# A fused linear-attention and two-layer kernel: the inputs of its first two groups laid out as token pairs, with tiled matmuls and a new hand-written order

## The chip, the cores and the metric

The kernel runs on one core of one Trainium2 chip. The metric is the device time of one launch in microseconds. Before the change three runs took 174.21, 173.97 and 174.07 us, median 174.07 us.

The engines are named as the profile names them: PE (matrix engine, with PEld for its weight loads), DVE (vector), ACT (scalar), POOL (GpSimd) and SP, which here only issues DMAs. Each engine runs its own queue of instructions strictly in order and waits on semaphores for the others.

## The reference

Two layers in a row. The first is a linear attention with a decaying state; for each batch `b`, head `h` and token `t`:

```python
B, H, S, D = 4, 8, 768, 48
for t in range(S):
    cur = einsum('bhd,bhe->bhde', u * k[t], v[t])
    y[t] = einsum('bhd,bhde->bhe', r[t], state + cur)
    state = w[:, :, None] * state + einsum('bhd,bhe->bhde', k[t], v[t])
```

`w` lies between 0.85 and 0.95, one value for each head and channel. The second layer takes `x`, the 3072 tokens with their 8 * 48 = 384 channels, through

```python
h = x @ w_in                       # 384 -> 2048
g = where(h >= 1, h, where(h <= -1, 0, (h + 1) ** 2 / 4))
out = g @ w_out                    # 2048 -> 384
```

All inputs and the output are float32 in DRAM; the matmuls run in bf16.

## The kernel before, in words

The tokens are cut into chunks of C = 128. A **unit** is one chunk of one batch, and a **group** is two units: the same chunk of two batches. There are 12 groups, g = 0 to 11, in order of chunk; groups 0 and 1 are chunk 0 of batches 0, 1 and of batches 2, 3. Unit n = 2g + j. Groups 0 and 1 have no state to read, since theirs is the first chunk.

For each group the attention is done in the chunked form. R, K and V are loaded with the token on the partition (`LR`, `LK`, `LV`, line 253), one 192-byte run for each token and head. `Rs` and `Ks` are R and K times powers of w (tables `Wup` and `Wdn`), in bf16; they are transposed, on PE for the first units (`TR`, `TK`, `T`) and by a DMA transpose later (`RT`, `KT`); `A` multiplies the transposes to 128 x 128 scores for each head; `AT` masks them with a triangular table on DVE; `Y` multiplies the masked scores by V and adds the state's part. The token's own term goes through `KU`, `RKU`, the sum `us` and the product `B`. `y` adds the two. `Sp`, `Tm`, `decayg` and `sbf` carry the state on. The result is transposed again, on PE (`X`, `xc`) for groups 0 to 2 and by a DMA transpose `xcg` (tile `xT`, line 467) from group 3.

The second layer runs in quarters q of 512 hidden channels for each group: `m g.q` is 12 matmuls into a pair of PSUM banks (tile `hp`, line 475), `r`, `s` (ACT, a few `r` on DVE) and `g` (DVE) are the activation, and `M g.jq` is four matmuls of unit j into the output's PSUM tile `op` (line 512). `og` copies a group's `op` to the SBUF tile `o` (line 112), which has four buffers, and `stg` stores it (line 558).

**What sets the order.** A long table of words, `ORDER`, is run through from left to right, and each engine's queue is the order in which the words issue its instructions; nothing reorders them later. `Z` words are matmuls on zeros whose result nobody reads (tile `z`, line 566); there are 60 of them. All loads, the DMA transposes and the stores are issued from SP in the order of the words; the weights `w_in` and `w_out` (`WI`, `WO`) are issued from POOL. PSUM is eight banks: two pairs `p0` and `p1` and, for the first two groups, four single banks, which become the pairs `p2` and `p3` later. A tile in a pair waits until the last reader of the pair's earlier tile is done.

The lines by which the steps below can be found: loads 253, DMA transposes 318 (`RT`, `KT`) and 467 (`xT`), scores 370, `Y` 432 and 438, `m` 475, `M` 512, copies of any kind 112, stores 558, and for the last group 539 and 555.

```python
def do_stg(e, b, g):
    nc.sync.dma_start(out=rows_out(g, 0, UNITS), in_=tiles["o", g])
```

Of the kernel before, what the change touches and what calls it, by code (L numbers as in the profile page):

```python
# [15 lines left out]
P = 128  # L16
# [23 lines left out]
M3.13 M3.03 xcg4 m4.0/1 LR7 KU5=G RKU5=G AT10 LK7 decayg3=G sbfg3=A Rs6=G og3=A us5 LV7 B5=G KU6=G RKU6=G r4.0 Sp8/2  # L40
Sp9 AT11 Tmg4 m4.1/3 s4.0=A Y10/0 Y11 yg5 m4.2/2 r4.1 g4.0 xcg5 RT6 s4.1=A g4.1 m4.3/0 r4.2 us6 KT6 r4.3 LV8 s4.2=A
g4.2 M4.00/1 M4.10 M4.01 stg0 M4.11 s4.3=A g4.3 m5.1/3 Ks7=G V7 M4.12 LR8 decayg4=G Rs7=G AA6/02 M4.02 M4.03 M4.13
r5.1 AT12 m5.0/0 s5.1=A V6 sbfg4=A stg2 AT13 Y12/2 Y13 stg1 og4=V m5.2/1 g5.1 KU8=G B6=G yg6 m5.3/3 KT7 xcg6 Sp10/2
r5.0 s5.0=A KU7=G RKU7=G r5.2 s5.2=A Sp11 g5.0 M5.00/0 M5.10 M5.11 M5.01 RT7 Tmg5 LR9 g5.2 M5.02 Ks8=G LK9 us7 r5.3
s5.3=A V8 g5.3 decayg5=G sbfg5=A LK11 m6.1/2 r6.1 s6.1=A stg3 Rs8=G RT8 B7=G AA7/13 M5.03 Rs9=G M5.12 M5.13 AT15
m6.0/3 og5=A r6.0 AT14 g6.1 Y14/0 Y15 yg7 RKU8=G KU9=G xcg7 s6.0=A m6.3/1 m6.2/2 g6.0 Sp12/0 Sp13 r6.3 r6.2 s6.2=A us8
KT8 M6.00/3 M6.10 M6.11 M6.01 Tmg6 LV11 B8=G s6.3=A m7.1/0 RT9 LK10 g6.2 M6.02 LV10 g6.3 AA8/21 M6.03 r7.1 M6.12 M6.13
decayg6=G AT16 sbfg6=A RKU9=G LR10 s7.1=A AT17 Ks9=G og6=A m7.0/2 Sp14/1 Sp15 Y16/3 Y17 r7.0 g7.1 m7.2/0 KU11=G s7.0=A
Tmg7 yg8 xcg8 Ks10=G KT9 r7.2 m7.3/1 g7.0 M7.00/3 s7.2=A g7.2 M7.10 M7.11 LV9 r7.3 M7.01 KU10=G s7.3=A g7.3 V10 stg6
decayg7=G M7.12 RKU10=G sbfg7=A M7.02 AA9/02 M7.13 m8.0/1 stg5 LR11 AT18 Rs10=G V9 KT10 M7.03 r8.0 s8.0=A AT19 RT10  # L50
og7=V us9 B9=G m8.1/0 m8.2/2 r8.1 s8.1=A Y18/3 Y19 stg7 g8.0 m8.3/1 yg9 r8.2 Rs11=G RKU11=G M8.00/3 M8.10 xcg9 g8.1
M8.11 s8.2=A g8.2 Sp16/0 Sp17 Tmg8 stg4 RT11 r8.3 s8.3=A M8.01 M8.02 g8.3 m9.0/2 r9.0 s9.0=A us10 decayg8=G AA10/01
AT21 Ks11=G M8.03 sbfg8=A B10=G AT20 M8.12 M8.13 g9.0 og8=A m9.1/1 Y20/0 Y21 r9.1 m9.2/3 s9.1=A yg10 xcg10 g9.1 r9.2
M9.00/0 m9.3/2 KT11 s9.2=A stg8 M9.10 M9.11 Sp18/1 Sp19 r9.3 g9.2 s9.3=A M9.01 Tmg9 M9.02 g9.3 m10.0/3 decayg9=G V11
us11 AA11/12 B11=G r10.0 s10.0=A AT23 M9.12 M9.03 M9.13 AT22 m10.1/2 g10.0 sbfg9=A Y22/1 Y23 og9=A r10.1 stg9 s10.1=A
yg11 xcg11 m10.3/0 M10.00/3 g10.1 M10.10 r10.3 m10.2/1 s10.3=A g10.3 r10.2 M10.11 M10.01 s10.2=A m11.0/2 g10.2 r11.0
# [18 lines left out]
def kernel(  # L75
# [82 lines left out]
    )  # L158
    wCm = const.tile([P, NP, 2 * D], F32, name="wCm")
# [53 lines left out]
    def do_Wup(e, b):  # L213
        t = tiles["up_t"] = pair(b[0], F32, "up_t")[:, 0, :DM]
        nc.scalar.activation(t, flat(tiles["lwp"]), AF.Exp, scale=up_col)

    def do_Wdn(e, b):
        t = tiles["dn_t"] = bank(b[0], [P, DM], F32, "dn_t")
        nc.scalar.activation(t, flat(tiles["lwp"]), AF.Exp, scale=dn_col)
# [30 lines left out]
    def load(x, what, cls, g, j):  # L250
        j0, j1 = by_unit(g, j)
        t = make(cls, (what, g), [P, UNITS * H, D], F32)
        nc.sync.dma_start(out=t[:, j0 * H : j1 * H, :], in_=source(x, g, j0, j1))
# [38 lines left out]
    def do_KU(e, b, g, j=None):  # L292
        product(e, make("KU", ("KU", g), [P, UNITS * H, D], F32), tiles["K", g], u_sb, g, j)
# [317 lines left out]
```

## Time and profile before

| | |
|---|---|
| median of three runs | 174.07 us (173.97 to 174.21) |
| span of the profiled execution, first to last instruction | 172.6 us |
| outside the span, by the median | about 1.5 us |
| PE busy | 164.4 us, 95% of the span, 1674 matmuls |
| DVE, ACT, POOL busy | 130.6, 129.9, 117.4 us |
| moved by DMA | 28.26 MB in 103,751 packets |

The page gives no other time for the profiled execution than its span, so sums are made against the span, and the 1.5 us around it are taken as unchanged. The page's first part is the busy time of each engine; the second cuts the span into 40 slices of 4.3 us; the third lists the DMA queues (q1 is SP's, q10 is ACT's, q0 is POOL's); the fourth follows the chain of work that ended last back from the end; the fifth groups instructions by line. Timelines give start and duration, then engine, line, operation and operands, and in brackets how long the engine stood idle before and what ended that.

### The profile page before, as it was taken

Reading aid. Unit: us, or ns where it says so; the run is one execution under the profiler, and the core shown is the slowest. Engines: PE = TensorE matmul, PEld = TensorE weight load, DVE = VectorE, ACT = ScalarE, POOL = GpSimd, SP = SyncE. Lnnn points to the kernel's source line nnn. Section 1 sums busy time; section 2 is a strip of 40 time slices with the busy share of each in tenths; the row PEclk is TensorE's granted clock in tenths of the full one; section 3 lists DMA queues with packets and bytes.
Section 4 is the critical chain, followed back from the end, with each engine's and each line's share of the span. In section 5 each row is a group of like instructions: output and inputs, shape, how many; then the busy total and the mean of one; then the engine's idle time right before and its main releaser. Section 6 shows DMA issues by size and latency. Waiting matters only on the chain.

```text
span 172.6 us, 4051 instructions
## 1 busy us (share of the span) xinstructions
PE 164.4 (95%) x1674; PEld 132.9 (77%) x1674; DVE 130.6 (76%) x150; ACT 129.9 (75%) x150; POOL 117.4 (68%) x86
## 2 busy tenths in 40 slices
PE   7989968999999999989999999999999999999991
PEld 5769868966889777588787797696897787888871
DVE  4578698988687688859789779885889959873752
ACT  4355698991699899189979879689695896988940
POOL 3496744998689949999999998999568804300000
PEclk9999999999999999999999999999999999999999
DMA  6999999998996999999999997998999025140022
GB/s 114 194 184 179 199 187 180 228 210 174 206 191 99 206 184 168 194 199 145 196 312 210 182 220 163 223 182 155 297 170 267 4 52 145 37 104 0 8 91 91
DMA packets 103751, 28.26 MB, mean 164 GB/s; under 512 B 98866, under 2 KB 102836, under 8 KB 103732
## 3 DMA queue, kind: packets, MB, share of 16 engines
q1 hardware_dynamic: 101824, 24.75, 79.9%
q0 software_dynamic: 1760, 3.15, 9.8%
q8 instruction: 13, 0.21, 0.6%
q10 hardware_dynamic: 148, 0.10, 0.2%
q14 instruction: 6, 0.05, 0.1%
HBM read 20.45 MB, written 4.72 MB: 146 GB/s over the span
## 4 chain that ended last, share of the span: by engine, by line
PE 87%; ACT 4%; DMA 2%; DVE 2%; issue 1%; POOL 0%; ACTq 0%; DVEq 0%
PE hp L475 35%; PE op L512 34%; PE A L370 4%; PE Y L438 3%; DMA xT<-y 2%; PE Y L432 2%; PE Sp L405 2%; PE z L566 2%; ACT pt L486 1%; PE T L330 1%; ACT TT L112 1%; PE lwp L207 1%; PE wp L233 1%; PE TR L330 1%; PE TK L330 1%
## 5 line engine op out<-in xcount | busy, mean ns | idle before, releaser
L475 PE MATMUL hp<-xT,w_in 128*128 128x256 bf16 x576 | 69.1, 273 | 1.3 <-DMA xT<-y 0.8
L512 PE MATMUL op<-w_out,g 128*128 128x384 bf16 (+1 forms) x400 | 68.4, 320 | 0.0
L498 DVE SCALAR_TENSOR_TENSOR g<-sq,hp 128x1024 bf16<-128x1024 bf16 x48 | 57.9, 1215 | 13.2 <-ACT sq L495 13.2
L475 PEld LDWEIGHTS <-w_in 128*128 128x128 bf16 x576 | 61.9, 114 | 4.6 <-issue 1.6
L486 ACT ACTIVATE pt<-hp 128x1024 f32<-128x1024 f32 x46 | 46.9, 1021 | 13.7 <-PE hp L475 13.7
L512 PEld LDWEIGHTS <-g 128*128 128x128 bf16 x400 | 37.5, 98 | 20.4
L495 ACT ACTIVATE sq<-pt 128x1024 bf16<-128x1024 f32 x46 | 48.3, 1057 | 1.2
L379 DVE TENSOR_TENSOR AT<-A,umask 128x1024 bf16<-128x1024 f32 x20 | 23.7, 1220 | 5.2 <-PE A L370 5.2
L282 POOL TENSOR_TENSOR Ks<-Ki,Wdn 128x768 bf16<-128x768 f32 (+1 forms) x12 | 20.3, 1689 | 8.5 <-ACT Wdn L225 3.4
L313 POOL TENSOR_TENSOR V<-Vb,diag 128x768 f32<-128x768 bf16 (+1 forms) x14 | 18.1, 1291 | 9.8 <-DVE diag L304 4.4
L282 POOL TENSOR_TENSOR RKU<-Ri,KU 128x768 f32<-128x768 f32 (+1 forms) x13 | 21.2, 1630 | 1.1 <-DVE KU L282 0.7
L282 POOL TENSOR_TENSOR KU<-Ki,u_sb 128x768 f32<-128x768 f32 (+1 forms) x13 | 21.2, 1634 | 0.4 <-DMA Ki<-in_k_dram 0.4
L416 POOL TENSOR_TENSOR state<-Tm,wCm 128x768 f32<-128x768 f32 x8 | 14.6, 1824 | 9.8 <-DVE Tm L413 9.8
L282 POOL TENSOR_TENSOR Rs<-Ri,Wup 128x768 bf16<-128x768 f32 x10 | 18.2, 1820 | 0.3 <-DMA Ri<-in_r_dram 0.3
L112 ACT CAST Vb<-Vi 128x768 bf16<-128x768 f32 (+1 forms) x14 | 10.2, 733 | 5.4 <-DMA Vi<-in_v_dram 5.4
L450 DVE TENSOR_TENSOR y<-Y,V 128x768 bf16<-128x768 f32 x10 | 9.6, 956 | 5.9 <-PE Y L438 3.3
L304 DVE TENSOR_REDUCE diag<-RKU 128x16 f32<-128x768 f32 (+1 forms) x14 | 11.6, 831 | 1.5 <-POOL RKU L282 1.5
L112 ACT CAST state_bf<-state 128x768 bf16<-128x768 f32 (+1 forms) x12 | 8.5, 717 | 4.4 <-POOL state L416 4.4
L112 ACT COPY o<-op 128x768 f32<-128x768 f32 (+1 forms) x9 | 6.7, 748 | 6.0 <-PE op L512 5.9
L438 PE MATMUL Y<-Vb,AT 128*128 128x48 bf16 x192 | 10.4, 186 | 0.4 <-ACT Vb L112 0.4
L438 PEld LDWEIGHTS <-AT 128*128 128x128 bf16 x192 | 9.5, 98 | 0.7 <-issue 0.5
L413 DVE TENSOR_TENSOR Tm<-Sp,state 128x768 f32<-128x768 f32 x8 | 7.7, 956 | 3.1 <-PE Sp L405 3.1
(73 smaller groups left out, 123.3 us busy)
## 6 DMA issues: line engine op xcount, KB each, us to landing
out_dram<-o SPq DMA_DIRECT2D x11, 384.0 KB, 3.8
Ki<-in_k_dram SPq DMA_DIRECT2D x9, 384.0 KB, 6.2
Ri<-in_r_dram SPq DMA_DIRECT2D x9, 384.0 KB, 6.2
Vi<-in_v_dram SPq DMA_DIRECT2D x9, 384.0 KB, 5.4
Ki<-in_k_dram SPq DMA_DIRECT2D x6, 192.0 KB, 4.0
Ri<-in_r_dram SPq DMA_DIRECT2D x6, 192.0 KB, 4.7
Vi<-in_v_dram SPq DMA_DIRECT2D x6, 192.0 KB, 6.0
w_in<-in_moe_w_in_dram POOLq DMA_DIRECT2D x2, 384.0 KB, 7.5
```

The source lines that it names most:

```text
L112: nc.scalar.copy(out, in_) if e == "A" else engines[e].tensor_copy(out, in_)
L282: engines[e].tensor_mul(part(out)[:, :, :, :D], part(a), rep(b, j1 - j0) if len(b.shape) == 3 and b.shape[1] == H else part(b))
L304: nc.vector.tensor_reduce(d[:, hs], tiles["RKU", g][:, hs, :], AX.X, ALU.add)
L313: engines[e].tensor_mul(t[:, hs, :], tiles["V", g][:, hs, :], tiles["diag", g][:, hs].unsqueeze(2).to_broadcast([P, n, D]))
L379: nc.vector.tensor_mul(t.rearrange("p i n t -> p (i n) t"), tiles["A", n].rearrange("p i (n t) -> p (i n) t", t=P), umask.unsqueeze(1).to_ ...
L416: engines[e].tensor_mul(states[g % BP], tiles["Tm", g], flat(wCm).unsqueeze(1).to_broadcast([P, UNITS, DM]))
L438: nc.tensor.matmul(Y[:, h * D : (h + 1) * D], AT[:, i, p, :], V[:, j * H + h, :], start=(c == 0), stop=True, skip_group_check=True,)
L475: nc.tensor.matmul(hp[:, f, :], w_in_sb[wi][:, i, wo * FG * P + f : (wo + 1) * FG * P : FG], tiles["xT", g][:, :, i, :], start=(i == 0), s ...
L486: nc.scalar.activation(t, tiles["hp", g, q], AF.Relu, bias=0.5, scale=0.5)
L495: nc.scalar.activation(t, p, AF.Square)
L498: nc.vector.scalar_tensor_tensor(out=make("g", ("g", g, q), [P, FG, TOK], BF16), in0=tiles["sq", g, q], scalar=1.0, in1=tiles["hp", g, q], ...
L512: nc.tensor.matmul(tiles[key][:, i, : o1 - o0], tiles["g", g, q][:, f, j * P : (j + 1) * P], w_out_sb[wi][:, wo, f * DO + o0 : f * DO + o1 ...
```

## The change

**Token pairs.** For groups 0 and 1 (`JOINT` = 2) the token's parity takes the place of the unit. Partition 64 b + q of the tile now holds tokens 2q and 2q + 1 of batch b, beside each other for each head, so that one run is 384 bytes instead of 192. A load still brings one batch of R, K or V, now into 64 partitions. `Rs`, `Ks`, `KU`, `RKU` and `V` for these groups read every second block of 48 (`beside`) and work on one parity of both batches, so each waits for both batches' loads. The power tables are made for each parity on ACT (`D0`, `D1`, `U0`, `U1`, in PSUM pairs 1 and 0) from new columns; the masks are two new tables, `pmask`, made on POOL and DVE at the start.

**Tiled matmuls.** In these two groups the 128 partitions hold two batches, so scores, `Y` and `Sp` are done on parts of the array. `A` of a unit is 16 matmuls of a 48 x 64 weight against 128 columns instead of 8; `Y` is 32 of 64 x 64 against 48 columns instead of 8 of 128 x 128; `Sp` is 8 of 64 rows instead of 4. `A` needs the transposed R of both parities and `Y` the masked scores of both.

**The output of these groups.** `rows_out` now gives, for g < 2, the rows of `out` as [batch, pair, 2 * 384]: 2 x 64 runs of 768 floats, where it gave 128 tokens x 2 batches x 384. The source is the same SBUF tile `o`.

**The rest.** All words of `ORDER` up to group 4 stand in a new order; from `m4.0` on the words are the same, with other PSUM pairs. 38 of the 60 zero matmuls are gone. In the last group each half of the output has a PSUM tile of its own, and its first half store is issued from SP instead of ACT. `g` has 12 buffers instead of 13, `TT` two instead of three.

On SP, from the store of group 0 (`stg0`) to the transposes of group 7's inputs; the names after `out_0_dram<-` are the `o` tiles of groups 0, 2 and 1, `xT` is `xcg6`. Before:

```order
L558 DMA out_0_dram<-o_790 128x2x384
L253 DMA Ri_1434<-in_r_dram 128x16x48
L558 DMA out_0_dram<-o_1103 128x2x384
L558 DMA out_0_dram<-o_894 128x2x384
L318 DMA_TRANSPOSE KT_1555<-Ks_92 128x8x128
L467 DMA_TRANSPOSE xT_1557<-y_1540 128x6x128
```

And after the change:

```order
L636 DMA out_0_dram<-o_912 2x64x768
L283 DMA Ri_1565<-in_r_dram 128x16x48
L636 DMA out_0_dram<-o_1235 128x2x384
L636 DMA out_0_dram<-o_1023 2x64x768
L366 DMA_TRANSPOSE KT_1686<-Ks_104 128x8x128
L543 DMA_TRANSPOSE xT_1688<-y_1671 128x6x128
```

Nothing moves here; the first and the fourth row, the stores of groups 0 and 1, have an outermost dimension of 2 in place of 128.

On DVE, the buffer that these stores free: the copy `og4`, the fifth user of the four `o` buffers. Before, with the semaphores that each row waits for (`DMAHW6_49` is that of `stg0`):

```order
L379 TENSOR_TENSOR AT_1470<-A_1438,umask_105 128x1024 [waits DVE_49,PE_49]
L379 TENSOR_TENSOR AT_1491<-A_1447,umask_105 128x1024 [waits PE_49]
L112 COPY o_1519<-op_1392 128x768 [waits DMAHW6_49,PE_49]
L498 SCALAR_TENSOR_TENSOR g_1534<-sq_1485,hp_1414 128x1024 [waits Activation_49]
L450 TENSOR_TENSOR y_1540<-Y_1493,V2_1538 128x768 [waits PE_49,Pool_49]
```

After:

```order
L439 TENSOR_TENSOR AT_1601<-A_1569,umask_117 128x1024 [waits DVE_49,PE_49]
L439 TENSOR_TENSOR AT_1622<-A_1578,umask_117 128x1024 [waits DVE_49,PE_49]
L115 COPY o_1650<-op_1523 128x768 [waits DMAHW6_49,PE_49]
L574 SCALAR_TENSOR_TENSOR g_1665<-sq_1616,hp_1545 128x1024 [waits Activation_49]
L526 TENSOR_TENSOR y_1671<-Y_1624,V2_1669 128x768 [waits PE_49,Pool_49]
```

The order is the same: the copy waits for the store of group 0, and behind it stands `y`, group 6's sum, which `xcg6` transposes.

At the start of ACT, from the logarithm of w on. Before:

```order
L203 ACTIVATE lnw_80<-w_row_69 1x8x48
L225 ACTIVATE Wdn_114<-lwp_149,dn_col_86 128x384
L219 ACTIVATE dn_t_174<-lwp_149,dn_col_86 128x384
L215 ACTIVATE up_t_183<-lwp_149,up_col_84 128x384
L112 COPY TT_192<-TK_178 128x512
```

After:

```order
L224 ACTIVATE lnw_80<-w_row_69 1x8x48
L237 ACTIVATE dn2_182<-lwp_180,dn2_col0_88 128x384
L237 ACTIVATE up2_184<-lwp_180,up2_col0_92 128x384
L115 COPY u_sb_139<-up_190 128x384
L237 ACTIVATE up2_184<-lwp_180,up2_col1_94 128x384
L237 ACTIVATE dn2_182<-lwp_180,dn2_col1_90 128x384
```

ACT now makes four tables and copies `u` (DVE did that before) ahead of the first copy of a transpose.

The diff, cut to its core:

```diff
     def load(x, what, cls, g, j):
         j0, j1 = by_unit(g, j)
         t = make(cls, (what, g), [P, UNITS * H, D], F32)
+        if g < JOINT:
+            nc.sync.dma_start(
+                out=t[j * HP : (j + 1) * HP].rearrange("q (h e) d -> q h (e d)", e=2),
+                in_=x[g * UNITS + j, :, :C, :].rearrange("h (q e) d -> q h (e d)", e=2),
+            )
+            return
         nc.sync.dma_start(out=t[:, j0 * H : j1 * H, :], in_=source(x, g, j0, j1))
...
+    def beside(x, i):
+        return x.rearrange("p (h e) d -> p e h d", e=2)[:, i]
...
     def do_Rs(e, b, g, j=None):
-        t = tiles["up_t"] if g == 0 and "up_t" in tiles else flat(Wup)
-        product(e, scaled("Rs", g), tiles["R", g], t.rearrange("p (h d) -> p h d", h=H), g, j)
+        if g < JOINT:
+            engines[e].tensor_mul(scaled("Rs", g)[:, j * H : (j + 1) * H, :D], beside(tiles["R", g], j), by_head(tiles["up2"][:, j, :DM]))
+        else:
+            product(e, scaled("Rs", g), tiles["R", g], Wup, g, j)
...
+                for j in range(UNITS):
+                    half = slice(j * HP, (j + 1) * HP)
+                    nc.tensor.matmul(
+                        A[i][half, p, :], by_parity(n)[rows, NP + p, half], tiles["TG", n // UNITS][rows, :, p, half],
+                        start=True, stop=True, skip_group_check=True,
+                    )
...
     def do_Y(e, b, n):
         g, j, c, bp = where(n)
         Y = half("Y", b, n)
+        if g < JOINT:
+            for h in range(H):
+                for i in range(2):
+                    for b in range(UNITS):
+                        rows = slice(b * HP, (b + 1) * HP)
+                        nc.tensor.matmul(
+                            Y[rows, h * D : (h + 1) * D], tiles["AT", UNITS * g + i][rows, h % 2, h // 2, j * HP : (j + 1) * HP], tiles["V", g][rows, i * H + h, :],
+                            start=(i == 0), stop=(i == 1), skip_group_check=True,
+                        )
+            return
...
     def rows_out(g, j0, j1):
         c, bp = divmod(g, BP)
+        if g < JOINT:
+            return out.rearrange("(b q e) d -> b q e d", q=S // 2, e=2)[bp * UNITS : (bp + 1) * UNITS, :HP]
         return out.rearrange("(b s) d -> s b d", s=S)[c * C : (c + 1) * C, bp * UNITS + j0 : bp * UNITS + j1, :]
...
     def half_out(e, g, j, i):
-        copy(e, make("o", ("o", g, j, i), [P, UNITS, DO], F32)[:, 0, : DO // 2], tiles["op", g, j][:, i, : DO // 2])
+        copy(e, make("o", ("o", g, j, i), [P, UNITS, DO], F32)[:, 0, : DO // 2], tiles["op", g, j, i][:, i, : DO // 2])
```

More of the change, by code (lines that the diff above doesn't have):

```diff
@@ L40 @@
[L40 to L44, printed above, removed]
@@ L211, in do_bu, with table, do_U, do_D @@
         nc.tensor.matmul(t, ones, u_row, start=True, stop=True)
[L213 to L219, printed above, removed]
+    def table(b, what, i, col):
+        if what not in tiles:
+            tiles[what] = pair(b[0], F32, what)
+        nc.scalar.activation(tiles[what][:, i, :DM], flat(tiles["lwp"]), AF.Exp, scale=col)
+    def do_U(e, b, i):
+        table(b, "up2", i, up2_col[i])
+    def do_D(e, b, i):
+        table(b, "dn2", i, dn2_col[i])
     def do_WupS(e, b):
@@ L307, in do_V @@
         t, hs = make("Vb", ("V", g), [P, UNITS * H, D], BF16), heads(g, j)
[L308 removed]
+        copy(e or "A", t[:, hs, :], beside(tiles["V32", g], j) if g < JOINT else tiles["V32", g][:, hs, :])
     def do_B(e, b, g, j=None):
@@ L403, in do_Sp @@
         for p in range(NP):
+            if g < JOINT:
+                rows = slice(j * HP, (j + 1) * HP)
+                for i in range(2):
+                    h = i * H + 2 * p
+                    nc.tensor.matmul(Sp[:, p, :], flat(tiles["Ks", g][rows, h : h + 2, :]), flat(tiles["V", g][rows, h : h + 2, :]), start=(i == 0), stop=(i == 1))
+                continue
             h = j * H + 2 * p
@@ L548, in do_o @@
         o = make("o", ("o", g, j), [P, UNITS, DO], F32)[:, 0]
-        copy(e, o, tiles["op", g, j][:, j, :DO])
+        copy(e, o, tiles["op", g, j, j][:, j, :DO])
     def do_og(e, b, g):
@@ L558, in do_stg, with idling, do_Zp @@
         nc.sync.dma_start(out=rows_out(g, 0, UNITS), in_=tiles["o", g])
-    def do_Zs(e, b):
-        tiles["z"] = pair(b[0], F32, "z")
+    def idling(t, n):
+        for i in range(n):
+            nc.tensor.matmul(t, idle[:, :P], idle[:, :P], start=True, stop=True)
     def do_Z(e, b, n):
-        for i in range(n):
-            nc.tensor.matmul(tiles["z"][:, 0, :P], idle[:, :P], idle[:, :P], start=True, stop=True)
-    def do_Zq(e, b, n):
-        for i in range(n):
-            nc.tensor.matmul(tiles["z"][:, 0, :D], idle[:, :P], idle[:, :D], start=True, stop=True)
+        idling(pair(b[0], F32, "z")[:, 0, :P] if later else bank(b[0], [P, P], F32, "z"), n)
+    def do_Zp(e, b, n):
+        idling(pair(b[0], F32, "z")[:, 0, :P], n)
     steps = {name[3:]: f for name, f in locals().items() if name.startswith("do_")}
```

138 lines of the change are left out of this document (90 added, 48 removed).

## The prediction

> **What bounds the kernel now.** I read the page's first and fourth part, then the timelines of SP, DVE and PE around the stores, and the DMA rows of short windows.
>
> ```profile
> PE 164.4 (95%) x1674; PEld 132.9 (77%) x1674; DVE 130.6 (76%) x150; ACT 129.9 (75%) x150; POOL 117.4 (68%) x86
> PE 87%; ACT 4%; DMA 2%; DVE 2%; issue 1%; POOL 0%; ACTq 0%; DVEq 0%
> DMA  6999999998996999999999997998999025140022
> ```
>
> PE is busy 95% of the span and carries 87% of the chain that ended last, so from the first `m` on whatever holds PE up is added to the end. The third row is the point of this case: the 16 DMA engines are nearly full until slice 31 (134 us). PE's slack is small, and so is the slack of what it waits for through the DMA queue.
>
> Where each stretch stands on PE, from the table of stretches (columns: stretch, its length, then busy us and instructions of PE, PEld, DVE, ACT, POOL; clock, DMA share, GB/s):
>
> ```profile
> 19.00:27.00 8.00, 6.42 (x86) 5.61 (x83) 7.38 (x13) 5.53 (x8) 4.08 (x6) 1.00 1.03 191
> 27.00:34.00 7.00, 6.73 (x62) 6.57 (x62) 6.55 (x9) 6.86 (x8) 5.14 (x4) 1.00 1.07 202
> 34.00:60.00 26.00, 26.00 (x275) 19.75 (x274) 19.94 (x21) 19.69 (x24) 23.20 (x14) 1.00 1.06 181
> ```
>
> PE is idle for 1.58 + 0.27 us between 19 and 34 us, and hardly after. So a faster start can win those 1.85 us and what the zero matmuls hold.
>
> **The change part by part. First, the stores of groups 0 and 1.** SP's timeline, in which the two stores stand with what is queued behind them, then the DVE copy that waits for the first, and two rows of PE:
>
> ```profile
> 83.64 1.57 SPq L558 DMA_DIRECT2D out_dram<-o  x1
> 85.26 0.46 SPq L253 DMA_DIRECT2D Ri<-in_r_dram  x1
> 85.77 2.76 SPq L558 DMA_DIRECT2D out_dram<-o  x2
> 88.62 2.21 SPq L318 DMA_TRANSPOSE KT<-Ks  x1
> 91.42 1.21 SPq L467 DMA_TRANSPOSE xT<-y  x1
> 88.44 0.96 DVE L112 COPY o<-op 128x768 f32<-128x768 f32 x1 [0.55 <-DMA out_dram<-o]
> 89.67 2.79 PE L475 MATMUL hp<-xT,w_in 128*128 128x256 bf16 x24
> 95.88 1.47 PE L475 MATMUL hp<-xT,w_in 128*128 128x256 bf16 x12
> ```
>
> The copy is `og4`. It already waits 0.55 us for `stg0`, since the fifth `o` tile takes the first one's buffer, and `m5.2`, the PE row at 89.67, needs the PSUM pair that it empties (it ends at 89.40). The `xT` row at 91.42 is `xcg6`, and `m6.1` at 95.88 needs it.
>
> How many DMA engines carry a transfer? Two rows of ACT's queue, the first from the window 0 to 16 us, in which it does two one-row loads (`w_row` and `u_row`), the second from 164 to 172 us, in which it does one store of 128 rows; then the rate of that last window in slices of 0.2 us:
>
> ```profile
> q10 hardware_dynamic: 4, 0.00, 0.1%
> ...
> q10 hardware_dynamic: 144, 0.10, 4.0%
> ...
> GB/s 0 0 0 0 284 376 369 376 369 192 0 0 0 0 0 0 0 0 0 0 0 0 0 0 0 0 0 0 0 138 369 369 296 327 315 154 0 0 0 0
> ```
>
> Two loads of one row make four packets: one of data and one completion each. The store makes 144: 128 rows and 16 completions. So a transfer with an outermost dimension of 1 ran on one engine, and one with 128 on sixteen. The changed stores have 2 at the destination and 128 at the source. No row shows a 2. The bounds are two engines and sixteen. I take two, since the 1 at one end was enough for one engine.
>
> The Trainium skill says the same (page DMA: Bandwidth & Descriptors, section Why a DMA increments its semaphore by 16 and not by 1): the number of engines is the largest up to 16 that divides the slowest dimension, other than 1, of both sides. By it 2 and 128 give two engines. The one-row loads and the 128-row store agree; a 2 no run has shown so far.
>
> Price: with sixteen engines the window runs at 369 to 376 GB/s, 23.3 for one, and a store of 384 KB (393,216 bytes) takes 1.05 us. On two engines each has 196,608 bytes: 8.4 us, 7.35 more. Bounds from the same row: 24 GB/s at its best gives 8.2; 296 on sixteen, 18.5 for one, gives 10.6.
>
> *First stall.* `og4` without its wait would start at 88.44 - 0.55 = 87.9. With `stg0` landing 7.35 later it starts at 95.8 and ends at 96.75, and `m5.2` starts there instead of 89.67: 7.1 us of PE, with `og4` blocking DVE and so group 6's `y` and `xcg6` behind it.
>
> *Second stall.* `stg1` is one of the pair at 85.77; the transposes `KT` and `xT` behind it use sixteen engines, so two of sixteen shares wait behind 8.4 us once more. When does `xT` land? From the window 83 to 98 us:
>
> ```profile
> DMA  9952599999999999999999994299999922999999
> ...
> xT<-y SPq DMA_TRANSPOSE x1, 3.4
> ```
>
> It lands at 91.42 + 3.4 = 94.8. On the two engines 14.7 us are added ahead of it, less the gap at slices 24 and 25 (0.375 us each, 40% and 20% busy), some 0.5. So 109.0, where `m6.1` started at 95.88: 13.1 us. `xcg6` is issued some 7 us later because of the first stall, near 98.5, still before the two engines come to it. So the two stalls are one chain and do not add: by the second, 13.1 us are lost in all, the first being contained in it. With 8.2 and 10.6 us for a store it is 12.7 and 17.5. Loads and `RT` behind `xT` slip too; `RT` (about 1.3 us in the queue) is hidden behind `m6.1`, the loads by the groups that lie between them and their use. Afterwards PE is the bound again and nothing gives the time back.
>
> **Second, PE after a stall.** The zero matmuls show the array at half pace at the start:
>
> ```profile
> 12.69 1.07 PE z L566 x9
> 17.27 0.22 PE z L566 x4
> ...
> 10.00:17.00 7.00, 6.62 (x77) 5.78 (x76) 5.77 (x11) 3.45 (x8) 5.46 (x7) 1.00 1.24 180
> ```
>
> 119 ns for one at 12.7 us, 55 ns at 17.3, although the clock column says 1.00 in the first stretch. An idle PE may fall back to that pace. After 34 us PE is never idle for long, so there are only bounds: nothing, or what the start shows, where PE was busy for 6.62 of the 7 us from 10 us on and still slow until about 17.3: 7.3 us at half pace, 3.7 lost. A slow stretch after the first stall is swallowed by the second; only what follows 109 us counts. I take 1.2, nearer nothing since PE works without gaps then.
>
> The Trainium skill (page TensorE: Matmul & The Clock Gate, Part 1) has the array at half clock after an idle window of some 3.4 us and back after a busy one; by that one window costs 1.7 us. The two rows agree with a factor of two; no row here shows a fall.
>
> **Third, the start.** Removed: 38 of 60 zero matmuls; half of the packets of twelve loads. Added: 144 matmuls in groups 0 and 1 (each of four units: `A` 8, `Y` 24, `Sp` 4 more), tables, and joint waits for both batches. Rows for the prices (from PE's timeline the first `m`, then a `Y` of a later group from its first matmul to the `m` that follows; from the chain of waits a pair of `A` and a first-group `Y`, and its shares by line):
>
> ```profile
> 19.21 1.50 PE L475 MATMUL hp<-xT,w_in 128*128 128x256 bf16 x12
> ...
> 51.62 0.21 PE L432 MATMUL Y<-state_bf,TT 128*128 128x96 bf16 x1
> ...
> 52.37 1.81 PE L475 MATMUL hp<-xT,w_in 128*128 128x256 bf16 x15
> ...
> 64.63 0.55 PE A L370 x16
> 14.94 0.32 PE Y L438 x8
> ...
> by line: PE hp L475 35.5%; PE op L512 34.4%; PE A L370 3.5%; PE Y L438 2.6%; DMA xT<-y 2.5%; PE Y L432 2.1%; PE Sp L405 1.7%; PE z L566 1.7%; ACT pt L486 1.1%; PE T L330 1.0%; ACT TT L112 1.0%; PE lwp L207 1.0%; issue 0.9%; PE wp L233 0.9%;
> ```
>
> 24 matmuls of a `Y` take 0.75 us, 31 ns each; 16 of an `A` 34 ns each; a `Y` in the slow stage 40 ns each. So 144 cost 4.5 us at full pace and 5.8 at half; a quarter of the array for one matmul may let two run at once, at best half of it, 2.3. Against it: 1.7% of 172.6 us are 2.9 us of zeros on the chain, and 1.85 us of idle PE, 4.7 together if all of it is won. Since ACT, ahead of its first copy, has six instructions in place of four, and each product waits for two loads, I don't count on more. So 4.5 to 5.8 lost against up to 4.7 won: from -2 (cheap matmuls, most of the gap won) to +3 (half pace, half won); I take +0.3.
>
> **Fourth, the end.**
>
> ```profile
> 169.49 0.36 DVE L112 COPY o<-op 128x192 f32<-128x192 f32 x1 [0.45 <-ACT o L112]
> ```
>
> The last DVE copy waits for ACT's of the other half; with PSUM tiles of their own both start together: -0.35. The other PSUM pairs, one `g` buffer fewer and the first half store's move to SP are taken at nothing: from 34 us on PE waits for no pair and no buffer, and the half stores are issued one after the other on either queue.
>
> **Sum.** Span 172.6 + 13.1 + 1.2 + 0.3 - 0.35 = 186.85; with the 1.5 us outside it, as in the median of 174.07, **188.3 us**.
>
> **The rivals.**
>
> *The stores keep sixteen engines, and the start gains.* Speaks for it: the source has 128 rows, and one side's shape might not be enough. Then the sum is 174.07 + 0.3 - 0.35, about 174.0, and with the cheap matmuls and the shorter loads at the start -2 - 0.35: 171.7, on the other side. It decides where the 384-byte loads let `m0.2` start before 18 us, against 19.2 for the first `m` before. Against: the two ACT rows. 5% for a gain, 3% for 174.0 within 0.35 us, 4% for a loss at the start alone (+2: 176).
>
> *Only the waiting copy loses.* The two engines carry the stores, but what is queued behind is not held up. Then 7.1 + 0.3 - 0.35, and 1.2 for the pace: 182.3. Against: one queue, and the third row at the top, that it is always full. 13%.
>
> *A store takes 10.6 us*, since these engines also carry their sixteenth of all loads: 17.5 in place of 13.1, 192.7. For it: the 296 GB/s in the last window. 10%.
>
> **How the numbers follow.** The forecast has 65%, the rivals 12, 13 and 10. The forecast's own bounds (12.7 us for the stores, and from nothing to 3.7 for the pace, from -2 to +3 for the start) and the two rivals at 182.3 and 192.7 set the range, 181.5 to 193; outside it lie the sixteen engines (12%) and a store that is slower still (8%). About 0.2%, 0.35 us, is what a measurement of this kernel can tell from no change (its three runs lie within 0.24). Faster by more: 0.06, the gain and a little for a loss that is smaller than I think. Within: 0.03. Slower: 0.91.
>
> **What would show each step.** In the changed kernel's profile: the DVE copy `o<-op` near 88 us waiting some 6 us or more for `out_dram<-o`; the store's median to landing over 9 us for two of them; PE's `hp` waiting for DVE's or its own PSUM pair near 90 us and for `xT<-y` near 100 us; the DMA share falling to two sixteenths in between; 14 completions fewer for each of the two stores in q1's packets. The matmuls right after at twice their time would show the pace. The prediction is wrong if those stores land in 4 us; then the start alone decides.

## The result and the profile after

The changed kernel takes 197.53 us (median of 4 runs, 196.72 to 198.24) against 174.14 (4 runs, 173.97 to 174.38) of the kernel before on the same chip: ratio 1.133, 95% interval 1.127 to 1.138. The forecast was 188.3 us with a range of 181.5 to 193.0. The direction is right; the time is 4.5 us above the range. The times of the experiments below are of runs in the fast state; one of the four runs of 3 and one of 4 were in the slower one and are left out.

The first and fourth part of the page of the changed kernel (span 195.3 us, 172.6 before):

```profile
PE 170.9 (88%) x1780; PEld 135.4 (69%) x1780; DVE 136.0 (70%) x165; ACT 129.2 (66%) x149; POOL 115.8 (59%) x86
PE 68%; DMA 14%; DVE 6%; SPq 4%; ACT 4%; issue 2%; ACTq 0%; DVEq 0%
```

PE was busy 95% of the span and is busy 88%; its part of the chain fell from 87% to 68%, and DMA's rose from 2% to 14%. So PE waits for transfers, and two places hold nearly all of it.

**Around the stores.** SP's, DVE's and PE's timelines of the changed kernel, the DMA busy row of the window 93 to 105 us (40 slices of 0.3 us), and from the page the clock that PE was granted (40 slices of 4.9 us):

```profile
93.46 1.02 SPq L636 DMA_DIRECT2D out_dram<-o  x1
95.62 9.29 SPq L636 DMA_DIRECT2D out_dram<-o  x2
105.01 6.89 SPq L366 DMA_TRANSPOSE KT<-Ks  x1
112.00 2.31 SPq L543 DMA_TRANSPOSE xT<-y  x1
...
104.56 0.96 DVE L115 COPY o<-op 128x768 f32<-128x768 f32 x1 [6.88 <-DMA out_dram<-o]
...
105.58 5.28 PE L551 MATMUL hp<-xT,w_in 128*128 128x256 bf16 x24 [5.97 <-DVE o L115]
116.78 1.54 PE L551 MATMUL hp<-xT,w_in 128*128 128x256 bf16 x12 [2.07 <-DMA xT<-y]
119.22 3.24 PE L588 MATMUL op<-w_out,g 128*128 128x384 bf16 x12
...
DMA  9997479999779999841111311111111111111116
...
PEclk9999999999999999999996696999999999999999
```

The DMA row shows the store of group 0 alone on the engines: a digit 1 is one to two tenths of sixteen engines, which fits two of them (0.13 in run 5), for some 6 us. The copy `og4` waits 6.88 us, `m5.2` behind it 5.97, `m6.1` 2.07 more for `xT`. The 24 matmuls after the first wait take 5.28 us where 24 took 2.79 before, and the 12 `op` after the second 3.24 (2.12 before); the clock row falls to 0.6 in the slices from 102.5 to 112.3 us and from 117.2 to 122.0.

**At the start.** The `w_in` loads on POOL, DVE, ACT and PE of the changed kernel:

```profile
8.77 0.94 POOL L268 DMA_DIRECT2D w_in<-in_moe_w_in_dram  x1
13.16 0.81 POOL L268 DMA_DIRECT2D w_in<-in_moe_w_in_dram  x1
...
8.94 0.56 DVE L322 TENSOR_TENSOR Rs<-Ri,up 128x384 bf16<-128x384 f32 x1 [4.95 <-DMA Ri<-in_r_dram]
19.43 0.56 DVE L322 TENSOR_TENSOR Rs<-Ri,up 128x384 bf16<-128x384 f32 x1 [5.95 <-DMA Ri<-in_r_dram]
19.91 2.48 DVE L444 TENSOR_TENSOR AT<-A,pmask 128x512 bf16<-128x512 f32 x4
...
21.85 0.93 ACT L115 CAST Vb<-Vi 128x384 bf16<-128x384 f32 x2 [6.84 <-DMA Vi<-in_v_dram]
...
13.13 1.39 PE L427 MATMUL A<-TG 48*64 48x128 bf16 x32
20.64 0.59 PE L378 MATMUL TR<-ident,Rs 128*128 128x128 bf16 x4 [6.12 <-DVE AT L444]
27.54 2.36 PE L551 MATMUL hp<-xT,w_in 128*128 128x256 bf16 x12
```

The first `m` starts at 27.54 us, 8.33 later than before. From 14.5 us on everything stands: DVE for the product `Rs1.0`, whose R is the 11th of the twelve loads, ACT for V, the 12th, and PE for DVE, which has the four `AT` products (their `A` is done at 14.5) queued behind `Rs1.0`.

Where the time went, by the start of three `m` on PE and by the span, in us:

| | before | after | difference |
|---|---|---|---|
| first `m` | 19.21 | 27.54 | 8.33 |
| `m5.1` | 87.61 | 97.40 | 9.79 |
| `m6.1` | 95.88 | 116.78 | 20.90 |
| span | 172.6 | 195.3 | 22.7 |

So the start costs 9.8 us, the stores 11.1, and what follows `m6.1` 1.8 more. The forecast had 0.3 for the start, 13.1 for the stores, and 1.2 less 0.35 for the rest.

### The profile page after: what moved, and what is told of

Read it like the earlier page. It is cut to its first block, busy times and chain, and to the rows that moved or that the text cites. A ratio compares the mean times of both kernels' runs of the same rounds, so it can differ in the third digit from the quotient of the medians.

```text
span 195.3 us, 4279 instructions
## 1 busy us (share of the span) xinstructions
PE 170.9 (88%) x1780; PEld 135.4 (69%) x1780; DVE 136.0 (70%) x165; ACT 129.2 (66%) x149; POOL 115.8 (59%) x86
## 4 chain that ended last, share of the span: by engine, by line
PE 68%; DMA 14%; DVE 6%; SPq 4%; ACT 4%; issue 2%; ACTq 0%; DVEq 0%
PE hp L551 29%; PE op L588 27%; DMA Vi<-in_v_dram 6%; DMA out_dram<-o 6%; SPq L278 4%; PE A L423 3%; DMA xT<-y 2%; ACT sq L571 2%; PE Y L500 2%; PE Y L514 2%; ACT pt L562 2%; PE Y L508 1%; PE Sp L471 1%; DVE g L574 1%; DVE AT L439 1%
## 5 line engine op out<-in xcount | busy, mean ns | idle before, releaser
L551 PE MATMUL hp<-xT,w_in 128*128 128x256 bf16 x576 | 72.7, 281 | 8.1 <-DVE o L115 6.0
L551 PEld LDWEIGHTS <-w_in 128*128 128x128 bf16 x576 | 63.2, 116 | 13.6 <-issue 6.6
L588 PE MATMUL op<-w_out,g 128*128 128x384 bf16 (+1 forms) x400 | 69.6, 323 | 0.0
L574 DVE SCALAR_TENSOR_TENSOR g<-sq,hp 128x1024 bf16<-128x1024 bf16 x48 | 58.0, 1216 | 13.1 <-ACT sq L571 13.1
L318 POOL TENSOR_TENSOR Ks<-Ki,Wdn 128x768 bf16<-128x768 f32 x10 | 18.3, 1825 | 13.3 <-PE Sp L471 9.2
L482 POOL TENSOR_TENSOR state<-Tm,wCm 128x768 f32<-128x768 f32 x8 | 15.3, 1908 | 8.2 <-DVE Tm L479 8.2
L318 POOL TENSOR_TENSOR KU<-Ki,u_sb 128x768 f32<-128x768 f32 x10 | 18.2, 1824 | 0.0
L318 POOL TENSOR_TENSOR RKU<-Ri,KU 128x768 f32<-128x768 f32 x9 | 16.4, 1823 | 0.3
L115 ACT CAST Vb<-Vi 128x768 bf16<-128x768 f32 (+1 forms) x13 | 9.7, 750 | 8.5 <-DMA Vi<-in_v_dram 8.4
L115 DVE COPY o<-op 128x768 f32<-128x768 f32 (+2 forms) x5 | 3.8, 756 | 8.8 <-DMA out_dram<-o 6.9
L322 DVE TENSOR_TENSOR Rs<-Ri,up 128x384 bf16<-128x384 f32 x4 | 2.2, 552 | 11.1 <-DMA Ri<-in_r_dram 10.9
```

The costliest lines, as they stand in the source:

```text
L115: nc.scalar.copy(out, in_) if e == "A" else engines[e].tensor_copy(out, in_)
L318: engines[e].tensor_mul(part(out)[:, :, :, :D], part(a), rep(b, j1 - j0) if len(b.shape) == 3 and b.shape[1] == H else part(b))
L482: engines[e].tensor_mul(states[g % BP], tiles["Tm", g], flat(wCm).unsqueeze(1).to_broadcast([P, UNITS, DM]))
L551: nc.tensor.matmul(hp[:, f, :], w_in_sb[wi][:, i, wo * FG * P + f : (wo + 1) * FG * P : FG], tiles["xT", g][:, :, i, :], start=(i == 0), s ...
L574: nc.vector.scalar_tensor_tensor(out=make("g", ("g", g, q), [P, FG, TOK], BF16), in0=tiles["sq", g, q], scalar=1.0, in1=tiles["hp", g, q], ...
L588: nc.tensor.matmul(tiles[key][:, i, : o1 - o0], tiles["g", g, q][:, f, j * P : (j + 1) * P], w_out_sb[wi][:, wo, f * DO + o0 : f * DO + o1 ...
```

## The experiments

The theory after the result: the two stores cost what the forecast said, because two DMA engines carry them; and the start is late because the last of its loads share the DMA engines with the 768 KB of `w_in`'s second half. The kernel before ran 174.07 to 174.49 us in these sessions.

**1. Split stores.** The same bytes in two DMAs of 64 rows each.

```diff
     def do_stg(e, b, g):
+        if g < JOINT:
+            for j in range(UNITS):
+                nc.sync.dma_start(out=rows_out(g, 0, UNITS)[j], in_=tiles["o", g][j * HP : (j + 1) * HP])
+            return
         nc.sync.dma_start(out=rows_out(g, 0, UNITS), in_=tiles["o", g])
```

> The changed kernel with each of the two stores of groups 0 and 1 split into two, one for each batch, so that the outermost dimension is 64 in place of 2. If the two stores cost what the traces say because two DMA engines carry them: the copy before m5.2 waits under 1 us for the store in place of 6.9, PE does not wait for xT before m6.1, and the span falls by the 11.1 us by which m6.1 slipped beyond the start's delay and some 1.7 us of slow matmuls: 195.3 - 12.8 = 182.5, time 184.7. If the halt near 105 us comes from the late start instead, which bunches loads and transposes in the queue, the shape changes little: over 194.

183.83 us (183.7 to 184.43), 13.7 less than the changed kernel; to before 1.054 (1.051 to 1.058). The DVE copy and `m6.1` in this kernel:

```profile
97.56 0.96 DVE L115 COPY o<-op 128x768 f32<-128x768 f32 x1 [0.55 <-DMA out_dram<-o]
...
105.01 1.47 PE L551 MATMUL hp<-xT,w_in 128*128 128x256 bf16 x12
```

The wait is 0.55 us again, as before the change, and `m6.1` comes 8.28 us after `m5.1` (96.73), as before (8.27). The first `m` is as late as ever, at 27.27.

**2. The stores alone, in the kernel before.**

```diff
     def rows_out(g, j0, j1):
         c, bp = divmod(g, BP)
+        if g < JOINT:
+            return out.rearrange("(b q e) d -> b q e d", q=S // 2, e=2)[bp * UNITS : (bp + 1) * UNITS, :HP]
         return out.rearrange("(b s) d -> s b d", s=S)[c * C : (c + 1) * C, bp * UNITS + j0 : bp * UNITS + j1, :]
```

> The kernel before, with nothing changed but the destination of the stores of groups 0 and 1: the same bytes as two batches of 64 rows of two tokens, outermost dimension 2 (so these output rows lie in other places than the reference has them). Two-engine theory: as forecast for the stores, 13.1 us and 1.2 of slow matmuls: 174.1 + 14.3 = 188.4, at least 186. If the stores' price needs the changed start as well: under 182. If the shape does nothing: 174.1.

187.36 us (187.01 to 188.34), ratio 1.075 (1.070 to 1.079): 12.9 us for this line alone. DVE and PE of this kernel, whose `m5.1` stands at 87.38:

```profile
94.74 0.96 DVE L112 COPY o<-op 128x768 f32<-128x768 f32 x1 [7.08 <-DMA out_dram<-o]
...
95.75 5.26 PE L475 MATMUL hp<-xT,w_in 128*128 128x256 bf16 x24 [6.16 <-DVE o L112]
107.34 2.48 PE L475 MATMUL hp<-xT,w_in 128*128 128x256 bf16 x12 [2.74 <-DMA xT<-y]
```

Both waits of the changed kernel, with nothing else changed. `m6.1` is 19.96 us behind `m5.1`, 11.7 more than before; the rest of the 13.0 us of span fits the half pace of the matmuls from `m6.1` on (12 in 2.48 in place of 1.47). So the two runs agree from both sides: the shape of the stores costs 12.9 to 13.7 us, wherever the start stands.

**3. The `w_in` load later.**

```diff
- ... LK2.1 WI2 KU0.0=G ... RKU0.0=G KU1.0=G WI0 AT1.0=V ...
+ ... LK2.1 KU0.0=G ... RKU0.0=G KU1.0=G WI2 WI0 AT1.0=V ...
```

> The changed kernel with one step moved: the 768 KB load of w_in's second half is issued by POOL three products later, right ahead of the next w_in load, so that it starts after the twelve loads of the first groups. Theory that this load, sharing the DMA engines with the last two of the twelve, is what makes R and V late: the 11th load lands near 14.5 us in place of 18.5, the first m starts near 22.5 in place of 27.5, and the time falls by 4 to 5 us to some 193. Rival, that the loads are late by themselves or that the matmuls and copies of the new layout fill the time: the first m stays after 26, time over 196.

193.32 us (192.3 to 193.58), 4.2 less. DVE's wait and the first `m`:

```profile
15.38 0.55 DVE L322 TENSOR_TENSOR Rs<-Ri,up 128x384 bf16<-128x384 f32 x1 [2.17 <-DMA Ri<-in_r_dram]
...
22.54 1.50 PE L551 MATMUL hp<-xT,w_in 128*128 128x256 bf16 x12
```

`Rs1.0` starts at 15.38 in place of 19.43, with the 11th load, and the first `m` 5.0 us sooner. Nothing was changed but the place of one load, so this load is the cause, and the packets in the traces show the sharing: in the changed kernel those of the 11th load lie between 13.4 and 18.5 us and those of the `w_in` load between 12.6 and 17.7, while in run 3 the 11th load has the engines to itself and takes 1.1 us (12.8 to 13.9). It leaves 3.3 us to the 19.21 of before.

**4. Both.**

```diff
+                nc.sync.dma_start(out=rows_out(g, 0, UNITS)[j], in_=tiles["o", g][j * HP : (j + 1) * HP])
...
- ... LK2.1 WI2 KU0.0=G ... KU1.0=G WI0 ...
+ ... LK2.1 KU0.0=G ... KU1.0=G WI2 WI0 ...
```

> The changed kernel with both, the split stores and the later w_in load. If the two causes are apart, as the difference of the spans by place says, the gains add: 197.5 - 12.8 - 4.5 = 180.2. If one feeds the other, the sum is not reached: over 182.

181.49 us (179.49 to 181.89): 2.3 less than with the split stores alone, not the 4.2 that the later load won by itself, and its runs lie wide. The first `m` here:

```profile
23.11 2.75 PE L551 MATMUL hp<-xT,w_in 128*128 128x256 bf16 x12 [0.56 <-DMA w_in<-in_moe_w_in_dram]
```

It now waits for `w_in` itself, and its 12 matmuls take 2.75 us where the profiled execution of run 3 had them at 1.50. So what is won at the start depends also on the pace of PE at that moment. Up to this `m` the two kernels run the same words on PE, within 0.2 us of each other; why one is at full pace here and the other only in its third `m` is not shown.

**5. DMAs alone.** A kernel of nothing but loads of r in five stages and four stores.

> DMAs alone, in stages kept apart by a clearing of the tiles; nothing of the reference is computed. Five stages of loads of r: six of 192-byte runs into 128 partitions (196,608 bytes each, as before), six of 384-byte runs into partitions 0 to 63 (as changed), the same six into the two halves by turns, three of 384-byte runs into 128 partitions (393,216 each), six of 192-byte runs into 64 partitions (98,304 each). Then four stores of 393,216 bytes with outermost dimension 2, 4, 8 and 16. Theory that the bytes set the pace: the first four stages take about as long, 6 x 1.08 = 6.5 us, and the fifth half of it. Rival, that the number of partitions written sets it: the stage into 128 partitions with 384-byte runs takes about half, 3.3 us, and the fifth as long as the second. Stores, if the outermost dimension gives the number of engines: 393,216 bytes at 24 GB/s an engine, 8.2, 4.1, 2.05 and 1.05 us.

Table of stretches of this kernel, one for each of the stages 1 to 4 and then the store with outermost dimension 2 (columns at the end: clock, DMA share of 16 engines, GB/s):

```profile
4.00:9.50 5.50, 4.74 (x8) 0.00 (x0) 1.00 1.03 204
9.60:15.20 5.60, 3.77 (x7) 0.00 (x0) 1.00 1.18 209
15.30:20.50 5.20, 3.98 (x7) 0.00 (x0) 1.00 1.25 221
20.60:23.80 3.20, 2.38 (x4) 0.00 (x0) 1.00 1.19 305
...
31.00:39.50 8.50, 2.22 (x4) 0.00 (x0) 1.00 0.13 47
```

The store is on 0.13 x 16 = 2.1 engines, at 47 GB/s: 8.5 us from its first to its last packet. The stores with 4, 8 and 16 took 6.9, 3.7 and 1.8 us; they fall in the expected order, but only the 2 has the expected size (4.1, 2.05 and 1.05 were expected), and why the 4 took 6.9 stays open. The Trainium skill's rule (DMA: Bandwidth & Descriptors, section Why a DMA increments its semaphore by 16 and not by 1), which the forecast named with no run of a 2, agrees with the share of this row. Loads: half the packets of twice the size bring nothing, 209 GB/s against 204, as long as they go to 64 partitions; into 128 partitions they run at 305. The fifth stage was held up by the clearing of its tiles and tells nothing.

**6. The stores on ACT's queue.**

```diff
     def do_stg(e, b, g):
-        nc.sync.dma_start(out=rows_out(g, 0, UNITS), in_=tiles["o", g])
+        (nc.scalar if g < JOINT else nc.sync).dma_start(out=rows_out(g, 0, UNITS), in_=tiles["o", g])
```

> The changed kernel with its two stores of outermost dimension 2 issued by ACT in place of SP. They still run on two engines, but the transposes on SP's queue no longer stand behind them in one queue. Theory that the second stall is the queue: the copy before m5.2 still waits some 7 us for the first store, and PE's wait for xT before m6.1, which adds 4 to 6 us, is gone: 192 to 194. Rival, that the two engines themselves are what xT waits for, whatever the queue: 196 to 198, as with SP.

197.82 us (two runs, 197.64 and 198.0): no gain. ACT's issue of the first store, then PE and DVE of this kernel:

```profile
89.43 0.62 ACTq L636 DMA_DIRECT2D out_dram<-o  x1
...
105.26 1.03 PE L423 MATMUL A<-RT,KT 48*128 48x128 bf16 x16 [11.41 <-DMA KT<-Ks]
...
110.01 0.96 DVE L115 COPY o<-op 128x768 f32<-128x768 f32 x1 [1.74 <-PE op L588]
```

My expectation fell, the rival stands, and in a form that it hadn't: the copy no longer waits for the store, but a transpose in SP's queue, `KT`, now lands 11.41 us late for PE. ACT issues the first of the stores at 89.43, 4.0 us sooner than SP did, and so ahead of this `KT` (90.62); the stall has moved with it. A transpose of another queue is held up as long, so it isn't the order in one queue that makes the transposes late. What they share with the store is the two engines; that each transpose needs its share on those two is the reading that fits, with no run of its own.

**7. The end alone, in the kernel before.** The key of the PSUM tile, as in the change, and two pairs for the last unit's halves.

```diff
-        key = ("op", g, j) if last else ("op", g)
+            key = ("op", g, j, i) if last else ("op", g)
...
- M11.10/0 ... M11.00/3
+ M11.10/03 ... M11.00/1
```

> The kernel before with only the end of the change: PSUM tiles of their own for the two halves of the last output. Forecast: the last DVE copy waits no more for ACT's, 0.35 us less, 173.7; the rival is that the copy starts earlier but the half stores end when they did: 174.1.

174.26 us (12 runs) against 174.4 (17 runs of before): ratio 0.9986, 0.9966 to 1.0005. DVE at the end of this kernel:

```profile
168.14 1.02 DVE L112 COPY o<-op 128x384 f32<-128x384 f32 x2 [1.27 <-PE op L511]
```

The two copies run on end, without the 0.45 us between them, and the profiled span is 172.2 us in place of 172.6. The step is seen in the trace; in the times it can't be told from nothing.

**8. The start rearranged further,** on top of 4.

```diff
- ... LR1.1 LV0.0 ... Rs1.0=V wC=A A0/01 ... KU1.0=G WI2 WI0 AT1.0=V TK3/0 Sp1/3 B0.1=G ... Y0/0 TR3/3
+ ... LV0.0 LR1.1 ... wC=A A0/01 ... KU1.0=G WI2 AT1.0=V Rs1.0=V TK3/0 Sp1/3 B0.1=G WI0 ... Y0/0 TR2/1 cR2=A TR3/3
```

> The kernel with split stores and the later w_in load, and its start rearranged further: R1.0's product goes behind the four A products in DVE's queue, its transposes behind the two Y, V's last load one place forward, and the second w_in load three POOL steps later. Theory that the product waiting for the 11th load held up the four A products (2.2 us of DVE's idle time in the run before) and that the two w_in loads together delayed the first m: A products from 13.6 us, first m near 21.5 and at full pace, time 1.5 to 2.5 us lower than with those two alone, about 179.5. Rival, that the rest of the start's loss is the work of the new layout itself: no gain, 181.5.

180.59 us (180.03 to 181.13) against 181.49 of 4 (179.49 to 181.89), which the times can't tell apart; the expected 179.5 is not reached. DVE's four `AT` and PE's first two `m`:

```profile
13.52 2.48 DVE L444 TENSOR_TENSOR AT<-A,pmask 128x512 bf16<-128x512 f32 x4 [0.30 <-PE A L427]
...
10.22 0.61 PE L378 MATMUL TK<-ident,Ks 128*128 128x128 bf16 x4 [2.38 <-DVE Ks L328]
22.22 2.75 PE L551 MATMUL hp<-xT,w_in 128*128 128x256 bf16 x12 [0.53 <-DMA w_in<-in_moe_w_in_dram]
25.47 1.56 PE L551 MATMUL hp<-xT,w_in 128*128 128x256 bf16 x12
```

The `AT` products now start at 13.52, 2.2 us sooner than in 4, but the first `m` only 0.9 sooner: it again waits for `w_in` and runs at half pace. And the first transposes stand at 10.22 where they stood at 7.8 before the change: their product needs R and K of both batches, four loads and a fifth ahead of them.

**9. The loads on two queues.** On top of 8: the loads of the second batch, into partitions 64 to 127, from ACT.

```diff
         if g < JOINT:
-            nc.sync.dma_start(
+            (nc.scalar if j else nc.sync).dma_start(
...
- LK1.0 LK0.1 LR0.1 ln=A Z20/0 ...
+ LK0.0 LR0.0 LV0.0 LK1.0 LR1.0 LV1.0 ln=A LK0.1 LR0.1 Z20/0 ... uS=A LV0.1 LK1.1 LR1.1 LV1.1 U1=A ...
```

> The kernel of the last start, with the loads of the second batch of each pair (partitions 64 to 127) issued by ACT, so that both halves of the partitions are written at once, in the order K, R, V of group 0 on each queue first; V0's casts go ahead of V1's and w_in's load two POOL steps earlier. Theory, from the stage alone, that a 196,608-byte load into 64 partitions takes about 1.0 us because only half of the partitions take it, and two halves at once 0.6 us each: the twelve loads have landed by 11.5 us in place of 15, the first m starts near 19 us, and the time is 2 to 3 us lower, near 178. Rival, that the bytes or the packets set the pace whatever the partitions: the twelve loads still end after 14 us and the time stays at 180 to 181.

181.5 us (180.41 to 181.96): no gain. Two stretches of this start:

```profile
2.50:8.00 5.50, 5.19 (x20) 3.63 (x17) 1.35 (x9) 2.36 (x5) 1.06 (x3) 1.00 1.19 217
8.00:11.00 3.00, 1.03 (x8) 0.77 (x8) 1.26 (x3) 0.83 (x2) 2.92 (x4) 1.00 1.34 179
```

217 and 179 GB/s with both halves of the partitions being written, against 192 and 176 in the changed kernel's first 10 us: the rival holds, the pace stays. The last of the twelve loads ends at 18.6 us and the first `m` starts at 24.23, 2.0 later than in 8.

**10. The pace of loads, cleaner.**

> Loads of r alone, nothing of the reference is computed. Six stages, each of 1,179,648 bytes in 384-byte runs and each after the one before has landed: (1) six loads into partitions 0 to 63, as changed; (2) three loads of double size into partitions 0 to 63; (3) six loads of four heads into 128 partitions; (4) three loads into 128 partitions with every second pair of tokens; (5) three loads into 128 partitions with neighbouring pairs; (6) the six of stage 1, the halves of the partitions by turns, on SP's and ACT's queues at once. Theory that 64 partitions take half of what 128 take: 1 and 2 some 5.7 us, 3, 4 and 5 some 3.6, 6 like 3. Rival, that the size of a load decides: 2, 4 and 5 are fast. Rival, that neighbouring bytes at the source decide (four pairs for each DMA engine with 64 partitions, eight with 128): 3 and 5 are fast, 4 is slow. The rearranged start with two queues speaks against stage 6 being fast: there the loads landed every 0.95 us.

The six stages in the table of stretches:

```profile
7.20:13.20 6.00, 1.58 (x3) 0.00 (x0) 1.00 1.06 197
15.10:21.00 5.90, 1.17 (x2) 0.00 (x0) 1.00 1.10 200
25.30:30.90 5.60, 1.03 (x2) 0.00 (x0) 1.00 0.82 211
33.10:37.40 4.30, 0.00 (x0) 0.00 (x0) 1.00 1.01 274
41.30:45.70 4.40, 1.32 (x2) 0.00 (x0) 1.00 1.01 268
49.30:54.90 5.60, 0.70 (x1) 0.00 (x0) 1.00 0.98 211
```

None of the three theories gives this pattern. Neighbouring bytes don't matter (4 like 5). Size alone doesn't (2 like 1), and the partitions alone don't (3 like 1): only large loads into 128 partitions are faster. In stage 3 the DMA share is 0.82, so there the issue of six loads may be the limit; that was not tried apart. The Trainium skill (SBUF — State Buffer, section Door 1: The DMA port swizzle) has partitions 0 to 63 reach half of the ports; stages 1 and 2 against 4 and 5 agree with it, while stage 3, 128 partitions at 211, shows next to nothing of it. Its advice to use one transfer of 128 partitions rather than two to the halves (DMA: Bandwidth & Descriptors, section Rules for kernel authors) agrees with stages 5 and 6, 268 against 211.

**11. The zeros taken out of the kernel before.** All `Z` words but the first two are left out of the order.

```diff
- ... AT0.1 Z4 A1/13 ... V0.0 Z9 TR3/1 ... us0.1 Z7 Y1/3 ... RKU1.0=G Z8 X0/2 Z4 TK2/3 ... xc1=A Z7 TK3/3
+ ... AT0.1 A1/13 ... V0.0 TR3/1 ... us0.1 Y1/3 ... RKU1.0=G X0/2 TK2/3 ... xc1=A TK3/3
```

> The kernel before with 39 of its 60 zero matmuls taken out, those after the first transposes, so that PE idles there as in the changed start. Theory that they hold the array at work until it goes to full pace at 17 us, and that a start without them runs its first m at half pace: full pace some 5 to 10 us later, time 1 to 2 us longer, 175 to 176. Rival, that the zeros stand in PE's way and that taking them out wins what they cost on the chain: 172 to 173.5.

176.65 us (175.83 to 177.12), ratio 1.0125 (1.0075 to 1.0174). PE's busy time in the stretch 10 to 17 us and its first two `m`:

```profile
10.00:17.00 7.00, 4.11 (x49) 2.95 (x48) 5.77 (x11) 3.45 (x8) 5.46 (x7) 1.00 1.27 184
...
19.71 2.74 PE L475 MATMUL hp<-xT,w_in 128*128 128x256 bf16 x12
22.72 1.50 PE L475 MATMUL hp<-xT,w_in 128*128 128x256 bf16 x12
```

PE is busy for 4.11 us of the 7 in place of 6.62, and the first `m` runs at half pace, as in the changed kernel. It starts only 0.5 us later than before, but by `m5.1` (89.33) 1.7 us are lost. So in the kernel before the zeros don't stand in the way; they pay 2.2 us. No run has the changed kernel with its 38 zeros put back. The Trainium skill (TensorE: Matmul & The Clock Gate, Part 1) has the array go to full pace after a busy window of some 3.4 us; the two kernels agree, though the profile's clock column shows 1.00 in this stretch in both.

## Why the prediction was right in part and missed the time

| first `m`, `m5.1`, `m6.1`, span | us |
|---|---|
| before | 19.21, 87.61, 95.88, 172.6 |
| after | 27.54, 97.40, 116.78, 195.3 |
| 1, split stores | 27.27, 96.73, 105.01, 181.9 |
| 2, before with the stores | 19.07, 87.38, 107.34, 185.6 |
| 3, later `w_in` | 22.54, 92.12, 111.53, 190.4 |
| 4, split and later | 23.11, 94.62, 102.89, 180.1 |
| 8, split, later, rearranged | 22.22, 92.99, 101.40, 178.2 |
| 9, as 8, loads on two queues | 24.23, 94.60, 102.87, 180.1 |
| 11, before without zeros | 19.71, 89.33, 98.03, 174.8 |

**First, the stores: right,** in cause and nearly in size. Two engines carried them, each store took 8.1 us from its first to its last packet after the change, 8.6 and 8.4 in run 2 (8.4 forecast), the copy was the first stall and `xT` the second, and the two did not add. Forecast 13.1 for the stalls, measured 11.1 after the change and 11.7 alone. Shorter stores explain at most 0.6 of the difference, and only after the change; the rest I put down to slack in the queue, for which I had 0.5 us. Two readings were off without harm: the 24 GB/s is not in the row named for it, whose best, 376, gives 23.5 for one engine; and the one-row loads were no support for the rule that the prediction cites, since their only dimension other than 1 is 384, which would give sixteen engines, and each went as one data packet. The support is run 5. One word was wrong: I had the transposes wait behind the stores in a queue. Run 6 shows that another queue doesn't help.

**Second, PE after a stall: right.** 1.8 us are lost behind `m6.1` after the change, with the gain at the end already taken off, and 1.5 in run 2 (1.2 forecast, 0 to 3.7 bounds). Run 1 has no stall there and 0.2. The fall that the prediction had only as a possibility stands in the clock row above.

**Third, the start: the step that failed.** Forecast +0.3, with -2 and +3 as bounds; measured +9.8 at `m5.1`. The term that I worked out, the matmuls, was too large rather than too small: 64 matmuls of a first-group `Y` take 1.90 us before full pace and 32 take 0.69 at it, 30 and 22 ns each, and I had used 31 to 40:

```profile
23.47 1.90 PE L500 MATMUL Y<-Vb,AT 64*64 64x48 bf16 x64
...
31.85 0.69 PE L500 MATMUL Y<-Vb,AT 64*64 64x48 bf16 x32
```

(both rows are of the changed kernel.) Since the 8 matmuls of a `Y` took 0.53 and 0.36 us at these two paces before, the 96 added ones cost 1.5 us, 16 ns each. What failed is what stood beside it: the joint waits are listed among what is added, but got no term ("each product waits for two loads, I don't count on more"), and no load got a landing time.

- Of the 9.8 us, 5.3 go with the place of the `w_in` load that shares the DMA engines with the 11th and 12th load (`m5.1` at 92.12 in run 3 against 97.40; with split stores 2.1, 94.62 in run 4 against 96.73 in run 1). They hold DVE's product, and behind it in the queue the four `AT`, and ACT's V.
- The first transposes, which wait for a pair of batches, start 2.2 us later (10.02 after the change against 7.8). How much of that reaches the first `m` is not shown; no run moved it.
- I entered the zeros as 2.9 us to be won. Run 11 shows that the sign was wrong in the kernel before, which loses 2.2 us without them. Run 8 gives the same picture, a first `m` of 2.75 us, and a loss that grows from 3.0 at the first `m` to 5.4 at `m5.1`.
- I let half the packets count for a possible gain. Runs 5 and 10 show none for loads into 64 partitions.

These parts overlap, since a later start also moves the moment at which PE comes to full pace; run 4 (2.3 us for the edit that won 4.2 in run 3) shows how loosely they add. That the late `w_in` load is a cause is shown; how the rest divides among the joint waits, the missing zeros and the added work stays open.

**Fourth, the end: right and too small to measure.** The wait is gone from the trace; run 7 gives 0.14% with an interval that reaches past nothing.

**The range.** Its top, 193.0, came from the store at 10.6 us (192.7), which no run showed, and from a start of at most +3. With a bound from the trace of before for a `w_in` load ahead of the last loads, 768 KB at the 180 to 190 GB/s that the start shows, 4.2 us, added to it, it would have stood at 197.2, still a little under the measured 197.5. Of the rivals, sixteen engines and a store of 10.6 us fell; of the one with only the copy's wait, the `xT` row (2.07 us of wait behind the copy's stall) shows that the second stall is real.

No version here beats the kernel before: the best of the changed line are run 8 at 1.036 (1.031 to 1.040) and run 4 at 1.037 (1.029 to 1.044), and run 7 can't be told from the kernel before.

## What to carry to other kernels

When an order of steps changes, give a landing time to each load that the first products need, in the order in which they are issued, with every other transfer that is issued before the last of them; a weight load moved ahead of two small loads cost 2 to 5 us here, nowhere near the lines that compute. Look at the outermost dimension of both sides of each DMA that is rewritten: a 2 there took fourteen of sixteen engines away, and cost 13 us through a buffer that came free late and through the transfers that came behind it. And before idle work is taken out, ask what pace the engine has without it.

## What was not expected of the hardware

- A load of 196,608 bytes takes as long in 384-byte runs into 64 partitions (197 to 209 GB/s) as in 192-byte runs into 128 (204), and both halves at once from two queues give 211; 268 to 305 came only from loads of 393,216 bytes into 128 partitions. The cause isn't settled.
- A store on two engines delays a transpose that another queue issues by as much as one of its own queue (run 6: 11.41 us at `KT`).
- A store with an outermost dimension of 4, 8 and 16 took 6.9, 3.7 and 1.8 us, with 2 8.5: less than in proportion from 2 to 4. One run, not explained.
